# A gated feed-forward layer in seven-product form: the last product of the first down projection divided once more

## The chip, the cores and the metric

One NeuronCore of a Trainium2 chip runs the whole kernel; there is no other core in it. The metric is the device time of one launch in microseconds. Before the change three runs gave 529.53, 529.77 and 530.21 us, median 529.77.

## The reference

```
def reference(x, w_gate, w_up, w_down):
    g = jnp.einsum("bsd,df->bsf", x, w_gate)
    u = jnp.einsum("bsd,df->bsf", x, w_up)
    h = _gelu(g) * u
    return jnp.einsum("bsf,fd->bsd", h, w_down)
```

x has 2048 rows of 1024 columns, the hidden width is 3584, all in bf16; `_gelu` is the tanh form. Three large matrix products, then, with a gate between the second and the third.

## The kernel before

**Seven products for eight.** A product of two matrices cut into 2 x 2 blocks is done with seven block products instead of eight. Sums of blocks of the left matrix (s1 to s4) and of the right one (t1 to t4) are made ahead, seven products are taken of blocks and sums, and the results are put together with adds. Sums are kept in a 32-bit form (`fp32r`), in which the matmuls then run.

**First part, up to about 350 us.** Gate and up projections, in two halves of 1024 rows (`NPASS` = 2, each of two blocks of 512 rows), over 28 blocks of 128 hidden columns. Here nearly all blocks are cut a second time, and GpSimd makes most of the sums. The products h leave for DRAM (`hd`), and sums of blocks of w_down too (`td`), since SBUF can't hold them.

**Second part: `down`, twice.** `down(0, ...)` does the first 1024 rows of the output, `down(1, ...)` the last 1024. In each, the left matrix h is four blocks h00, h01, h10, h11 (`h[kh][c]`: kh the half of the hidden width, c the block of 512 rows), each 14 tiles (`NJ`) of 128 hidden columns by 512 rows. Its stages follow each other on TensorE:
- two raw products in bf16, h00 and h10 with the raw left columns of w_down (`chunk`, `rows`, L707 to L733); the raw columns come in chunks of two tiles: `fetch12` puts one chunk into a slot, `fetch_early` four chunks into one of the two `w` tiles.
- two products of sums, s2 with t2 and s1 with t1 (L735 to L744); VectorE makes s1 and s2 (`make12`), t1 and t2 are loaded from `td` (`load12`).
- two more, s3 with t3 and s4 with the raw right columns (L746 to L757); VectorE makes s3, t3 and s4 (`make73`), from raw columns that `fetch73` loads; ACT casts the raw ones (`tb`).
- the last product, the block h11 with t4, which is loaded from `td` by `load4`.

Only the last stage differs between the two calls. In the first, h11 is cast on ACT tile by tile (`make_sa`), and 14 tiles by four row blocks, 56 matmuls of 512 columns, go into the banks `e`, which ACT then copies out (`put21`, L759). In the second, `inner_product` (L638) cuts this product once more into seven, over 7 tiles (`H`) and 256 columns (`Q`): each of the seven is 14 matmuls of 256 columns, 98 in all. Its left sums s1 to s4 are four VectorE adds of 128 x 1792 (`inner_sums`), of which s1 and s2 lie in the tiles `xT` and s3 and s4 in the two `w` tiles. Its right sums are 28 GpSimd adds of 128 x 256: `inner_t` (t1, then t2 from it, seven times), `inner_t3` (seven) and `inner_t4` (seven). `inner_cast` casts h11 on ACT.

**What sets the order.** SP (which issues all DMAs), VectorE, GpSimd and TensorE run in the order in which the code is written (`tc.manual_schedule`), and every wait holds up all that stands behind it on its engine. In `down`, `step(n)` is called ahead of each piece of TensorE's work and runs what an agenda has for that n: `at` holds for both halves, `at_tail(last, ...)` for one. So `at_tail(1, 50 + 1.3 * t, inner_t, t)` puts the sums of tile t at step 50 + 1.3t of the second half. `more_0` has the loads of h for the second half, at steps 56, 59, 61 and 63 of the first, and the two `fetch_early` at step 46.

**Room.** 59 slots of 2 KB per partition (`kpool`) are handed out in turn; a tile that gets a slot waits until its last reader is done. The `w` pool has two tiles. SP has at most eight DMAs under way: each waits for the landing of the eighth before it. `even`, `odd`, `cc`, `dd` are pairs of the eight PSUM banks; `e` and `c` of `down` are four banks each, and change places between the halves.

All DVE sums go through `dve` (L94), all GpSimd sums through `pool` (L97), all matmuls of this part through `matmul` (L115), so these are the lines that the profile names; tiles tell them apart.

```
def dve(out, a, b, op):
    nc.vector.tensor_tensor(out=out, in0=a, in1=b, op=op)

def pool(out, a, b, op):
    nc.gpsimd.tensor_tensor(out=out, in0=a, in1=b, op=op)
```

Of the kernel before, what the change touches and what calls it, by code (L numbers as in the profile page):

```python
# [10 lines left out]
def kernel(  # L11
# [10 lines left out]
    nc = tc.nc  # L22
    ENG = mybir.EngineType
    ORDER = {ENG.SP, ENG.DVE, ENG.Pool, ENG.PE}
    P = nc.NUM_PARTITIONS
# [15 lines left out]
    NJ = NFB // 2  # L41
# [14 lines left out]
    AT12 = [0, 0, 1, 2, 4, 5, 9, 12, 16, 18, 22, 27, 29, 31], [4, 4, 8, 8, 12, 12, 15, 16, 18, 20, 22, 27, 29, 31]  # L56
    AT12S = [6, 7, 9, 10, 13, 14, 16, 18, 20, 23, 25, 27, 29, 31]
    EARLY = 8
    AT73 = [31 + 2 * j if j < 7 else 38 + j for j in range(NJ)]

    ctx.enter_context(tc.manual_schedule(engines=ORDER))
# [472 lines left out]
        tb = cast(rr[:, 1, :], "tb")  # L534
        q73[j] = s3, t3, s4, tb

    def make_sa(j):
        sa[j] = cast(h[1][1][:, j, :], "sa")

    def fetch12(n):  # L540
        kh, j = n // 7, 2 * (n % 7)
        if (1, n) in raw:
# [10 lines left out]
            raw[1, n] = big[:, n - n0]  # L553
            nc.sync.dma_start(out=raw[1, n], in_=wdn[:, kh, j : j + 2, :N])

    def inner_sums(late):
        hi = h[1][1][:, :H], h[1][1][:, H:]
        a11, a21 = hi[0][:, :, :Q], hi[0][:, :, Q:]
        a12, a22 = hi[1][:, :, :Q], hi[1][:, :, Q:]
        if not late:  # L560
            s1, s2 = [xpool.tile([P, H, Q], f32r, name=f"xT{n}") for n in range(2)]
            dve(s1, a21, a22, ADD)
            dve(s2, s1, a11, SUB)
            return s1, s2
        s3, s4 = [wpool.tile([P, H, Q], f32r, name="w") for _ in range(2)]
        dve(s3, a11, a21, SUB)
        dve(s4, a12, inner[1], SUB)
        return s3, s4

    def inner_t(t):  # L570
        b1, b2 = q4[t], q4[H + t]
# [27 lines left out]
    for j in range(NJ):  # L599
        at(AT12S[j], make12, j)  # L600
        at(AT73[j] - 4, fetch73, j)
        at(AT73[j], make73, j)
    sa, it, inner = {}, {}, []
    tails = {}, {}

    def at_tail(last, step, what, j):
# [4 lines left out]
    for j in range(NJ):  # L611
        for last in range(2):
            if last or j not in STAY:
                at_tail(last, AT12[last][j], lambda j, last=last: load12(j, BIG12[last]), j)
        at_tail(0, 49 + 0.65 * j, load4, j)
        at_tail(0, 54 + 0.55 * j, make_sa, j)
    for t in range(H):
        for j in (t, H + t):
            at_tail(1, 47 + 1.3 * t, load4, j)
        at_tail(1, 50 + 1.3 * t, inner_t, t)  # L620
        at_tail(1, 59, inner_t3, t)
        at_tail(1, 60, inner_t4, t)
        at_tail(1, 53 + 1.1 * t, inner_cast, t)

    def load_h(p, kh, c, j0, j1):
        nc.sync.dma_start(out=h[kh][c][:, j0:j1], in_=hd[p, kh, c][:, j0:j1])
# [8 lines left out]
        r0 = (2 * ip + c) * N + i * P  # L635
        nc.sync.dma_start(out=out2[r0 : r0 + P, dc * N : (dc + 1) * N], in_=st)

    def inner_product(ip, e, c, ss):  # L638
        zz = [hpool.tile([P, 2, N], f32, name=f"h{n}0") for n in range(2)]
        z1, z6, z7, z5 = [b.rearrange("p (r q) -> p r q", r=2) for b in c]  # L640
        T = range(H)
        a11 = [sa[t] for t in T]
        a12 = [sa[H + t][:, :Q] for t in T]
        a22 = [sa[H + t][:, Q:] for t in T]
        b11, b21 = [[q4[h + t][:, :Q] for t in T] for h in (0, H)]
        b22 = [q4[H + t][:, Q:] for t in T]
        t1, t2, t3, t4 = [[it[t][n] for t in T] for n in range(4)]
        s1, s2, s3, s4 = [[s[:, t] for t in T] for s in ss]

        def go(out, lhs, rhs, fresh=False, rs=R2):  # L650
            for r in rs:
                for t in T:
                    matmul(
                        out(r), lhs[t][:, r * P : (r + 1) * P], rhs[t],
                        fresh and r == 0 and t == 0, t == H - 1,
                    )

        left, right = slice(0, Q), slice(Q, N)

        def put(i):  # L660
            r0 = (2 * ip + 1) * N + i * P
            st = slot([P, N], bf16, "st")
            dve(st, e[i], zz[i // 2][:, i % 2], ADD)
            nc.sync.dma_start(out=out2[r0 : r0 + P, :N], in_=st)

        go(lambda r: e[r][:, right], s4, b22, rs=range(1))
        go(lambda r: z1[:, r], a11, b11, True)
        nc.scalar.copy(out=zz[0][:, :, left], in_=z1)
        go(lambda r: z6[:, r], s2, t2, True)
        u2 = new(dve, z6, zz[0][:, :, left], ADD, "sum", [P, 2, Q], f32)  # L670
        go(lambda r: z7[:, r], s3, t3, True)
        dve(zz[1][:, :, left], z7, u2, ADD)
        go(lambda r: z5[:, r], s1, t1, True)
        dve(zz[0][:, :, right], z5, u2, ADD)
        go(lambda r: e[r][:, right], s4, b22, rs=range(1, 2))
        go(lambda r: e[r][:, left], a12, b21, rs=range(1))
        put(0)
        dve(zz[1][:, :, right], z5, zz[1][:, :, left], ADD)
        go(lambda r: e[r][:, left], a12, b21, rs=range(1, 2))
        put(1)  # L680
        for r in R2:
            go(lambda r: e[2 + r][:, left], a22, t4, rs=range(r, r + 1))
            put(2 + r)

    def down(ip, e, c, last, more):
        I = range(NS)

        def step(n):
            todo(n, last)
            if last and n in (20, 44):  # L690
                inner.extend(inner_sums(n == 44))
            more(n)

        def chunk(kh, j):
            n = kh * 7 + j // 2
            got = raw[1, n][:, j % 2, :]
            if j % 2:
                raw.pop((1, n))
            return got

        def rows(ps, lhs, rhs, start, stop, some=I):
            for i in some:
                matmul(ps[i], lhs[:, i * P : (i + 1) * P], rhs, start, stop)

        step(-1)
        held = []
        for j in range(NJ):  # L707
            step(j)
            held.append((j, chunk(0, j)))
            if j < NJ - SEAM and (last or j >= SEAM):  # L710
                for some in (I[:2], I[2:]):
                    for k, rhs in held:
                        rows(e, h[0][0][:, k, :], rhs, k == 0, False, some)
                held = []
        for i in I:
            for k, rhs in held:
                rows(e, h[0][0][:, k, :], rhs, False, k == NJ - 1, [i])
            nc.scalar.copy(out=c[i], in_=e[i])
        held = []
        for j in range(NJ):  # L720
            step(NJ + j)
            held.append((j, chunk(1, j)))
            if j == 1:
                for i in I:
                    for k, rhs in held:
                        rows(c, h[1][0][:, k, :], rhs, False, False, [i])
            if j > 1:
                for k, rhs in held:
                    rows(c, h[1][0][:, k, :], rhs, False, k == NJ - 1)
            if j > 0:  # L730
                held = []
        for i in I:
            store(ip, 0, i, 0, lambda st: nc.scalar.copy(out=st, in_=c[i]))  # L733

        for t in range(NJ + LAG):  # L735
            step(2 * NJ + t)
            if t < NJ:
                rows(e, s12[t][1], q12[t][1], False, t == NJ - 1)
            if t == NJ - 1:
                u2 = [snap(e[i], "u2") for i in I]  # L740
            if t >= LAG:
                j = t - LAG
                rows(c, s12[j][0], q12.pop(j)[0], j == 0, j == NJ - 1)
        p5 = [snap(c[i], "p5") for i in I]  # L744

        for t in range(NJ + LAG):  # L746
            step(3 * NJ + LAG + t)
            if t < NJ:
                rows(e, q73[t][0], q73[t][1], False, t == NJ - 1)
            if t == NJ - 1:  # L750
                for i in I:
                    store(ip, 1, i, 1, lambda st: dve(st, e[i], p5[i], ADD))
            if t >= LAG:
                j = t - LAG
                rows(c, q73[j][2], q73[j][3], False, j == NJ - 1)
        for i in I:
            store(ip, 0, i, 1, lambda st: dve(st, c[i], u2[i], ADD))  # L757

        def put21(i):  # L759
            store(ip, 1, i, 0, lambda st: nc.scalar.copy(out=st, in_=e[i]))  # L760

        if last:
            for j in range(NJ):
                step(4 * NJ + 2 * LAG + j)
            inner_product(ip, e, c, inner)
        else:
            for j in range(NJ):
                step(4 * NJ + 2 * LAG + j)
                rows(e, sa[j], q4[j], False, j == NJ - 1)
            for i in I:  # L770
                put21(i)


    warm = nc.const_aps.tensor(1.0, [P, N], bf16)
# [346 lines left out]
    def more_0(step):  # L1121
# [2 lines left out]
            load_h(0, 1, 1, 8, NJ - 1)  # L1124
        if step == 32:
            store_made(NJ - 1)
        if step in (56, 59, 61):
            kh, c = {56: (0, 0), 59: (1, 0), 61: (0, 1)}[step]
            new_h(kh, c)
            for j0, j1 in ((0, 4), (4, 8), (8, NJ)):  # L1130
                load_h(1, kh, c, j0, j1)
        if step == 46:
            fetch_early(0), fetch_early(4)
        if step == 63:
            new_h(1, 1)
            for j0, j1 in ((0, 4), (4, 8), (8, NJ)):
                load_h(1, 1, 1, j0, j1)

    E = [E[0][1], E[0][0], E[1][0], E[1][1]]
    down(0, E, F[0] + F[1], False, more_0)  # L1140
    down(1, F[0] + F[1], E, True, lambda step: None)

# [28 lines left out]
```

## Time and profile before

| | us |
|---|---|
| median of three runs | 529.77 |
| the profiled execution | 528.81 |
| its span, first to last instruction | 527.0 |
| TensorE busy | 520.1 |
| VectorE busy | 384.8 |
| GpSimd busy | 329.6 |
| ACT busy | 290.9 |
| second part, first half begins | 349 |
| its last product, begin and end | 424.07, 436.76 |
| second half's last product begins | 511.75 |

The span is 1.8 us shorter than the execution's time, which has a start and an end around it. The granted TensorE clock is 0.999 of full speed over the span. The 16 DMA engines are busy nearly without a break from 399 us to 471 us, at up to 420 GB/s.

How to read the lines: PE is TensorE's matmuls, PEld its weight loads, DVE VectorE, POOL GpSimd, SPq the DMA issues of SyncE. A line of the timeline gives start, length, engine, line of the code, operation, output <- inputs by the names of the tiles, shape, and how many instructions were put together in it; in brackets how long the engine was idle before and what ended that. Recorded lengths of matmuls overlap: the distance of their starts tells what one costs. Recorded lengths of VectorE and GpSimd adds overlap a little too, by 0.04 to 0.09 us where one follows another at once.

### The profile page before, as it was taken

To read this page: it belongs to the slowest core of one execution; us is meant where nothing else is said; L and a number is where in the kernel's file an instruction comes from. 1 tells how busy PE (TensorE), PEld (TensorE's weight loads), DVE (VectorE), ACT (ScalarE), POOL (GpSimd) and SP (SyncE) were. 2 spreads that over 40 slices of the span, in tenths; PEclk is the share of its full clock that TensorE was granted. 3 is DMA by queue.
4 is the path that set the end of the run, shared out by engine and by line. 5 is a ranking of instruction groups with operands and counts; after the bars stand their busy time and mean duration, and the time that the engine had idled before them with its cause. 6 is when DMAs were issued, how large, how long until landed. Compare 5 with 4: busy or idle time off the path is not lost.

```text
span 527.0 us, 7930 instructions
## 1 busy us (share of the span) xinstructions
PE 520.1 (99%) x2362; PEld 368.4 (70%) x2393; DVE 384.8 (73%) x586; ACT 290.9 (55%) x535; POOL 329.6 (63%) x339
## 2 busy tenths in 40 slices
PE   8999999999999999999999999999999999999997
PEld 4568686867667676767676676754788884488887
DVE  2984636427889889898978889897789226976933
ACT  2555655656778687868787786851135602133430
POOL 1179959998899999999999999840000000000494
PEclk9999999999999999999999999999999999999999
DMA  9785244131625357363827455999997999983741
GB/s 249 160 191 125 76 131 119 41 109 58 204 80 180 108 194 222 111 205 126 255 91 229 148 173 159 332 372 416 385 294 224 400 350 375 394 297 113 227 135 61
DMA packets 104906, 106.96 MB, mean 203 GB/s; under 512 B 19744, under 2 KB 82976, under 8 KB 104864
## 3 DMA queue, kind: packets, MB, share of 16 engines
q1 hardware_dynamic: 104864, 106.46, 62.1%
q8 instruction: 19, 0.31, 0.2%
q14 instruction: 23, 0.19, 0.1%
HBM read 73.66 MB, written 29.62 MB: 196 GB/s over the span
## 4 chain that ended last, share of the span: by engine, by line
PE 96%; DMA 2%; DVE 1%; issue 0%; SPq 0%; ACT 0%; ACTq 0%; DVEq 0%
PE bank L115 96%; DMA hd<-h 1%; DMA xn<-in_x_dram 1%; DVE bank L94 0%; SPq L783 0%; DVE h L94 0%; DVE kz L94 0%; DVE st L94 0%; PE bank L790 0%; ACT u L111 0%; ACT ky L111 0%; DVE v L94 0%; ACTq L111 0%; DVEq L94 0%
## 5 line engine op out<-in xcount | busy, mean ns | idle before, releaser
L115 PE MATMUL bank<-h,s 128*128 128x512 f32 x492 | 129.3, 394 | 0.0
L97 POOL TENSOR_TENSOR q<-q 128x256 fp32r<-128x256 f32 x28 | 24.3, 901 | 145.9 <-PE bank L115 145.4
L115 PE MATMUL bank<-xT,w 128*128 128x512 bf16 (+1 forms) x448 | 106.0, 376 | 1.4
L115 PEld LDWEIGHTS bank<-h,s 128*128 128x128 f32 x492 | 92.3, 188 | 20.9 <-ACT u L111 0.5
L115 PEld LDWEIGHTS <-w 128*128 128x128 bf16 x504 | 45.7, 98 | 59.0 <-issue 10.6
L97 POOL TENSOR_TENSOR s<-w 128x512 fp32r<-128x512 bf16 (+1 forms) x74 | 75.9, 1041 | 17.6 <-DMA w<-in_w_gate_dram 10.5
L115 PE MATMUL bank<-t,s 128*128 128x512 f32 x276 | 75.5, 399 | 0.3 <-ACT u L111 0.3
L115 PE MATMUL bank<-q 128*128 128x512 f32 x264 | 65.6, 390 | 0.0
L115 PEld LDWEIGHTS bank<-t,s 128*128 128x128 f32 x276 | 51.6, 188 | 12.8 <-ACT u L111 1.0
L111 ACT COPY p<-bank 128x512 f32<-128x512 f32 x76 | 42.8, 588 | 29.2 <-PE bank L115 28.6
L115 PEld LDWEIGHTS bank<-q 128*128 128x128 f32 x264 | 49.6, 188 | 10.4
L111 ACT COPY u<-bank 128x512 f32<-128x512 f32 x62 | 36.0, 592 | 30.4 <-PE bank L115 27.7
L94 DVE TENSOR_TENSOR q<-h,h 128x512 fp32r<-128x512 bf16 x56 | 38.4, 685 | 15.4 <-DMA h<-hd 15.4
L97 POOL TENSOR_TENSOR s<-s,s 128x256 fp32r<-128x256 f32 x57 | 42.2, 762 | 1.5
L115 PEld LDWEIGHTS <-h 128*128 128x128 bf16 x224 | 21.7, 98 | 26.5 <-issue 0.5
L94 DVE TENSOR_TENSOR xz<-bank,xz 128x512 f32<-128x512 f32 x40 | 27.5, 691 | 16.9 <-PE bank L115 11.0
L97 POOL TENSOR_TENSOR s<-w,s 128x512 fp32r<-128x512 bf16 (+1 forms) x36 | 39.1, 1102 | 0.6 <-ACT sh L106 0.6
L97 POOL TENSOR_TENSOR s<-s,w 128x512 fp32r<-128x512 f32 (+1 forms) x36 | 36.6, 1035 | 0.8
L97 POOL TENSOR_TENSOR m<-raw,m 128x512 fp32r<-128x512 bf16 x28 | 34.5, 1232 | 2.2
L106 ACT CAST tb<-raw 128x512 fp32r<-128x512 bf16 x28 | 16.8, 632 | 30.7 <-DMA raw<-in_w_down_dram 23.9
L94 DVE TENSOR_TENSOR h<-g,bank 128x512 bf16<-128x512 f32 x42 | 28.6, 685 | 6.7 <-ACT g L209 3.5
L94 DVE TENSOR_TENSOR bank<-bank,u 128x512 f32<-128x512 f32 x47 | 32.4, 688 | 0.0
(117 smaller groups left out, 907.9 us busy)
## 6 DMA issues: line engine op xcount, KB each, us to landing
raw<-in_w_down_dram SPq DMA_DIRECT2D x68, 256.0 KB, 3.9
q<-td SPq DMA_DIRECT2D x66, 256.0 KB, 5.4
hd<-h SPq DMA_DIRECT2D x110, 128.0 KB, 1.7
td<-m SPq DMA_DIRECT2D x42, 256.0 KB, 2.3
h<-hd SPq DMA_DIRECT2D x17, 512.0 KB, 6.9
out_dram<-st SPq DMA_DIRECT2D x32, 128.0 KB, 3.6
h<-hd SPq DMA_DIRECT2D x5, 768.0 KB, 9.4
w<-in_w_gate_dram SPq DMA_DIRECT2D x7, 512.0 KB, 4.4
```

The lines of the kernel that those rows point to most:

```text
L94: nc.vector.tensor_tensor(out=out, in0=a, in1=b, op=op)
L97: nc.gpsimd.tensor_tensor(out=out, in0=a, in1=b, op=op)
L106: nc.scalar.copy(out=t, in_=src)
L111: nc.scalar.copy(out=t, in_=ps)
L115: nc.tensor.matmul(ps, lhsT=lhs, rhs=rhs, start=start, stop=stop, skip_group_check=True)
```

## The change

The first half's last product takes the form of the second's: 98 matmuls of 256 columns through `inner_product`, with a branch of its own there, instead of 56 of 512.
- Sums: `load4`, `inner_t`, `inner_t3`, `inner_t4` and `inner_cast` now stand on both agendas, at the same steps; `make_sa` and `put21` go. `inner_sums` becomes `inner_sum(n)`, one sum per call. In the first half sums 0 and 1 are made at step 54, 2 and 3 inside `inner_product`, between VectorE's adds there. In the second half they stay at steps 20 and 44.
- Partial results (`zz`) of the first half go into four slots instead of two `h` tiles, and `put` adds each output block in two halves of 256 columns.
- Loads for the second half: the two `fetch_early` at step 46 become four `fetch12` at step 55. `fetch_early(4)`, the loads of h01 and h11 and three further `fetch12` are issued by `late_loads`, inside `inner_product`, where the tile of sum 2 has to come free first. The loads of h00 and h10 stay at steps 56 and 59.
- Order of the seven in the first half: a12 b21, a11 b11, s2 t2, s1 t1, s3 t3, s4 b22, a22 t4.

```diff
+    INNER = {54: (0, 1)}, {20: (0, 1), 44: (2, 3)}
...
-        at_tail(0, 49 + 0.65 * j, load4, j)
-        at_tail(0, 54 + 0.55 * j, make_sa, j)
     for t in range(H):
+        for last in range(2):
+            for j in (t, H + t):
+                at_tail(last, 47 + 1.3 * t, load4, j)
+            at_tail(last, 50 + 1.3 * t, inner_t, t)
+            at_tail(last, 59, inner_t3, t)
+            at_tail(last, 60, inner_t4, t)
+            at_tail(last, 53 + 1.1 * t, inner_cast, t)
...
+            zz = [[slot([P, 2, Q], f32, "z") for _ in R2] for _ in R2]
...
+                for n in R2:
+                    dve(st[:, sides[n]], e[i][:, sides[n]], zz[i // 2][n][:, i % 2], ADD)
...
+        if not ip:
+            go(lambda r: e[r][:, left], a12, b21)
+            go(lambda r: z1[:, r], a11, b11, True)
+            nc.scalar.copy(out=zz[0][0], in_=z1)
+            go(lambda r: z6[:, r], s2, t2, True)
+            inner_sum(2)
+            u2 = new(dve, z6, zz[0][0], ADD, "sum", [P, 2, Q], f32)
+            inner_sum(3)
+            go(lambda r: z5[:, r], s1, t1, True)
+            dve(zz[0][1], z5, u2, ADD)
+            go(lambda r: z7[:, r], s3, t3, True)
+            dve(zz[1][0], z7, u2, ADD)
+            late_loads()
+            dve(zz[1][1], z5, zz[1][0], ADD)
+            go(lambda r: e[r][:, right], s4, b22)
+            for i in range(2):
+                put(i)
+            for r in R2:
+                go(lambda r: e[2 + r][:, left], a22, t4, rs=range(r, r + 1))
+                put(2 + r)
+            return
...
-        if step == 46:
-            fetch_early(0), fetch_early(4)
+        if step == 55:
+            for n in range(4):
+                fetch12(n)
...
+    def late_loads():
+        fetch_early(4)
+        for kh in range(2):
+            new_h(kh, 1)
+            for j0, j1 in ((0, 4), (4, 8), (8, NJ)):
+                load_h(1, kh, 1, j0, j1)
+        for n in range(EARLY, EARLY + 3):
+            fetch12(n)
```

More of the change, by code (lines that the diff above doesn't have):

```diff
@@ L535, in make73 @@
         q73[j] = s3, t3, s4, tb
-    def make_sa(j):
-        sa[j] = cast(h[1][1][:, j, :], "sa")
     def fetch12(n):
@@ L554, in fetch_early, with inner_sum @@
             nc.sync.dma_start(out=raw[1, n], in_=wdn[:, kh, j : j + 2, :N])
-    def inner_sums(late):
+    def inner_sum(n):
         hi = h[1][1][:, :H], h[1][1][:, H:]
@@ L559, in inner_sums @@
         a12, a22 = hi[1][:, :, :Q], hi[1][:, :, Q:]
[L560 to L568, printed above, removed]
+        if n < 2:
+            inner[n] = xpool.tile([P, H, Q], f32r, name=f"xT{n}")
+        else:
+            inner[n] = wpool.tile([P, H, Q], f32r, name="w")
+        a, b, op = ((a21, a22, ADD), (inner[0], a11, SUB), (a11, a21, SUB), (a12, inner[1], SUB))[n]
+        dve(inner[n], a, b, op)
     def inner_t(t):
@@ L602 @@
         at(AT73[j], make73, j)
-    sa, it, inner = {}, {}, []
+    sa, it, inner = {}, {}, [None] * 4
     tails = {}, {}
@@ L614 @@
                 at_tail(last, AT12[last][j], lambda j, last=last: load12(j, BIG12[last]), j)
-        at_tail(0, 49 + 0.65 * j, load4, j)
-        at_tail(0, 54 + 0.55 * j, make_sa, j)
     for t in range(H):
[L618 to L623, printed above, removed]
+        for last in range(2):
[5 more added lines that the diff above has]
+            at_tail(last, 53 + 1.1 * t, inner_cast, t)
     def load_h(p, kh, c, j0, j1):
@@ L636, in store, with inner_product @@
         nc.sync.dma_start(out=out2[r0 : r0 + P, dc * N : (dc + 1) * N], in_=st)
-    def inner_product(ip, e, c, ss):
-        zz = [hpool.tile([P, 2, N], f32, name=f"h{n}0") for n in range(2)]
+    def inner_product(ip, e, c):
+        if ip:
+            z = [hpool.tile([P, 2, N], f32, name=f"h{n}0") for n in range(2)]
+            zz = [[t[:, :, :Q], t[:, :, Q:]] for t in z]
+        else:
+            zz = [[slot([P, 2, Q], f32, "z") for _ in R2] for _ in R2]
         z1, z6, z7, z5 = [b.rearrange("p (r q) -> p r q", r=2) for b in c]
@@ L647, in inner_product @@
         t1, t2, t3, t4 = [[it[t][n] for t in T] for n in range(4)]
-        s1, s2, s3, s4 = [[s[:, t] for t in T] for s in ss]
+        s1, s2, s3, s4 = range(4)
         def go(out, lhs, rhs, fresh=False, rs=R2):
+            if isinstance(lhs, int):
+                lhs = [inner[lhs][:, t] for t in T]
             for r in rs:
@@ L658, in inner_product @@
         left, right = slice(0, Q), slice(Q, N)
+        sides = left, right
         def put(i):
@@ L662, in put @@
             st = slot([P, N], bf16, "st")
-            dve(st, e[i], zz[i // 2][:, i % 2], ADD)
-            nc.sync.dma_start(out=out2[r0 : r0 + P, :N], in_=st)
+            if ip:
+                dve(st, e[i], z[i // 2][:, i % 2], ADD)
+            else:
+                for n in R2:
+                    dve(st[:, sides[n]], e[i][:, sides[n]], zz[i // 2][n][:, i % 2], ADD)
+            nc.sync.dma_start(out=out2[r0 : r0 + P, :N], in_=st)
+        if not ip:
[19 more added lines that the diff above has]
+            return
         go(lambda r: e[r][:, right], s4, b22, rs=range(1))
         go(lambda r: z1[:, r], a11, b11, True)
-        nc.scalar.copy(out=zz[0][:, :, left], in_=z1)
+        nc.scalar.copy(out=zz[0][0], in_=z1)
         go(lambda r: z6[:, r], s2, t2, True)
-        u2 = new(dve, z6, zz[0][:, :, left], ADD, "sum", [P, 2, Q], f32)
+        u2 = new(dve, z6, zz[0][0], ADD, "sum", [P, 2, Q], f32)
         go(lambda r: z7[:, r], s3, t3, True)
-        dve(zz[1][:, :, left], z7, u2, ADD)
+        dve(zz[1][0], z7, u2, ADD)
         go(lambda r: z5[:, r], s1, t1, True)
-        dve(zz[0][:, :, right], z5, u2, ADD)
+        dve(zz[0][1], z5, u2, ADD)
         go(lambda r: e[r][:, right], s4, b22, rs=range(1, 2))
@@ L677, in inner_product @@
         put(0)
-        dve(zz[1][:, :, right], z5, zz[1][:, :, left], ADD)
+        dve(zz[1][1], z5, zz[1][0], ADD)
         go(lambda r: e[r][:, left], a12, b21, rs=range(1, 2))
@@ L689, in step @@
             todo(n, last)
-            if last and n in (20, 44):
-                inner.extend(inner_sums(n == 44))
+            for some in INNER[last].get(n, ()):
+                inner_sum(some)
             more(n)
@@ L757, in down @@
             store(ip, 0, i, 1, lambda st: dve(st, c[i], u2[i], ADD))
[L759 to L771, printed above, removed]
+        for j in range(NJ):
+            step(4 * NJ + 2 * LAG + j)
+        inner_product(ip, e, c)
     warm = nc.const_aps.tensor(1.0, [P, N], bf16)
@@ L1126, in more_0 @@
             store_made(NJ - 1)
-        if step in (56, 59, 61):
-            kh, c = {56: (0, 0), 59: (1, 0), 61: (0, 1)}[step]
-            new_h(kh, c)
+        if step in (56, 59):
+            kh = int(step == 59)
+            new_h(kh, 0)
             for j0, j1 in ((0, 4), (4, 8), (8, NJ)):
-                load_h(1, kh, c, j0, j1)
-        if step == 46:
-            fetch_early(0), fetch_early(4)
-        if step == 63:
-            new_h(1, 1)
+                load_h(1, kh, 0, j0, j1)
+        if step == 55:
+            for n in range(4):
+                fetch12(n)
+    E = [E[0][1], E[0][0], E[1][0], E[1][1]]
+    def late_loads():
+        fetch_early(4)
+        for kh in range(2):
+            new_h(kh, 1)
             for j0, j1 in ((0, 4), (4, 8), (8, NJ)):
-                load_h(1, 1, 1, j0, j1)
-    E = [E[0][1], E[0][0], E[1][0], E[1][1]]
+                load_h(1, kh, 1, j0, j1)
+        for n in range(EARLY, EARLY + 3):
+            fetch12(n)
     down(0, E, F[0] + F[1], False, more_0)
```

## The prediction

> **What bounds the kernel now.** I read the page first (busy shares, then the chain that ended last), then the timeline of each engine from 395 us on, where the change lies, then the landings of the DMAs there.
>
> ```profile
> PE 520.1 (99%) x2362; PEld 368.4 (70%) x2393; DVE 384.8 (73%) x586; ACT 290.9 (55%) x535; POOL 329.6 (63%) x339
> PE 96%; DMA 2%; DVE 1%; issue 0%; SPq 0%; ACT 0%; ACTq 0%; DVEq 0%
> ```
>
> TensorE is the bound: 99% busy, 96% of the chain, and its timeline shows no idle time from 350 us to 523 us. So a matmul removed is time won, and any wait put into TensorE's queue is time lost at full price. The stage that changes is the last product of the first half, 424.07 to 436.76, 12.69 us; the form it takes on is that of the last product of the second half.
>
> ```profile
> 420.44 3.79 PE L115 MATMUL bank<-tb,q 128*128 128x512 f32 x16
> 424.07 12.85 PE L115 MATMUL bank<-q,sa 128*128 128x512 f32 x56
> 436.76 13.99 PE L115 MATMUL bank<-w,h 128*128 128x512 bf16 x62
> ```
> ```profile
> 511.75 0.99 PE L115 MATMUL bank<-q,w 128*128 128x256 f32 x7
> 512.58 1.84 PE L115 MATMUL bank<-q,sa 128*128 128x256 f32 x14
> ...
> 520.03 3.52 PE L115 MATMUL bank<-q,sa 128*128 128x256 f32 x28
> ```
>
> Starts are what count in these rows: 56 matmuls of 512 columns in 12.69 us are 0.227 each. In the second half 98 matmuls of 256 columns begin at 511.75 and the last one begins at 520.03 + 3.52 - 0.28 (its own length) = 523.27: 97 steps in 11.52 us, 0.119 each, a little over half of 0.227.
>
> **Part 1, TensorE's work.** 56 x 0.227 = 12.69 us go, 98 x 0.1188 = 11.64 us come: **-1.05 us**, and no more than that is to be had. Without any new wait the products would begin at: a12*b21 424.1, z1 425.7, z6 427.4, z5 429.1, z7 430.7, s4*b22 432.4, a22*t4 434.0, end 435.7.
>
> **Part 2, the sums on GpSimd.** The 28 sums of `inner_t`, `inner_t3`, `inner_t4` are new in this half, where GpSimd is idle from 349 us on. They are those of the second half, which the trace shows. From the second sum on (500.09) to the end of the last (519.65) they take 19.56 us: 1.51 per pair while t2 waits for t1, 0.70 each for the 14 of t3 and t4, 0.74 for one alone. The first one is the row that decides this case:
>
> ```profile
> 494.76 5.25 POOL L97 TENSOR_TENSOR q<-q 128x256 fp32r<-128x256 f32 x1 [145.35 <-PE bank L115]
> ```
> ```profile
> 498.13 0.69 DVE L94 TENSOR_TENSOR q<-raw 128x512 fp32r<-128x512 bf16 x1
> 498.73 0.69 DVE L94 TENSOR_TENSOR q<-h,q 128x512 fp32r<-128x512 bf16 x1
> ```
>
> It takes 5.25 us instead of 0.74. VectorE then runs the sums of `make73`, one every 0.60 us without a gap, each with both inputs in SBUF, and ends at 499.41; GpSimd's sum ends 0.60 us behind that. So GpSimd did not get in while they ran. The reverse is seen where the first projections run:
>
> ```profile
> 155.25 2.29 POOL L97 TENSOR_TENSOR s<-s,w 128x512 fp32r<-128x512 f32 x2
> 156.39 1.70 DVE L94 TENSOR_TENSOR h<-v,v 128x512 bf16<-128x512 f32 x1
> 157.50 1.61 POOL L97 TENSOR_TENSOR s<-w,s 128x512 fp32r<-128x512 bf16 x1
> ```
>
> `h<-v,v` (two SBUF inputs) needs 0.69 alone; here it ends 0.55 behind the GpSimd sum that was running (157.54), and the next GpSimd sum is 0.5 longer than its usual 1.1. One waits for the other; VectorE adds that read PSUM, such as the one at 158.01, run beside GpSimd.
>
> When may GpSimd start? In the built program its first sum waits for a buffer that matmul 32 of the 112 of the stage before frees: 398.67 + 32 x 0.227 + 0.2 = 406.1 (in the second half it is matmul 36: 486.35 + 36 x 0.227 + 0.2 = 494.7; the row says 494.76). The q loads that it reads land earlier than it needs them: the loads of the stage no longer stand behind eight `w` loads (398.83 to 403.21 on SP). From 406.1 I add up what the two engines must do one at a time:
> - the rest of `make73` on VectorE, 406.1 to 410.1: 4.0
> - `inner_sum(0)` and `(1)`, put right behind it: 2 x 2.02 (the `xT<-h` rows at 451.25 and 453.31), 4.05
> - the 28 GpSimd sums, 0.74 + 19.56 = 20.3
> - `inner_sum(2)` and `(3)`, which the change sets **between** the products on VectorE, behind the u stores (426.07) and behind u2 (429.9): 4.05.
>
> 406.1 + 32.4 = **438.5** for the last t4 sum. Who gets in first does not change this sum. In order of time: second GpSimd sum at 414.8, t2 complete at 424.6 (needed 427.4), five t3 sums by 430.1 around `inner_sum(2)`, then `inner_sum(3)` to 432.1, the last t3 at 433.5, t4 433.5 to 438.4. In the second half none of this hurts, since all four inner sums are over at 486.8, before GpSimd starts.
>
> **TensorE behind it.** z7 begins at 430.7, waits for t3 until 433.5 and ends at 434.5 instead of 432.4. s4*b22 runs to 436.2 (its `inner_sum(3)` is there at 432.1). a22*t4 takes its seventh matmul after 438.4 and then seven more: 438.4 + 0.12 + 0.83 = **439.4**. The second half so begins 2.65 us later than at 436.76.
>
> **Part 3, loads, queue, the rest.** SP's queue now holds `late_loads` until z7 has ended (the tile of `inner_sum(2)` has to come free): 434.6. Behind it wait four chunks of w_down, six of h, three more chunks. From an idle queue the first lands 2.5 us after issue (471.14 to 473.8); then a landing each 0.70 us for 256 KB, 1.27 for 512 KB, 1.9 to 2.45 for 768 KB (landings between 403 and 442). Chunk 8 lands at 434.6 + 2.5 + 3 x 0.70 + 9.5 + 0.70 = 449.4; TensorE wants it 13.83 us into the half (450.59 - 436.76), at 453.2: 3.8 us of cover. The first `make12` starts some 7 us later than its 438.85, its product is wanted at 463.4. With what stands behind on the queue the first raw chunk of `make73` lands near 471 instead of 464.7, that is 3.6 us later against TensorE; VectorE has 3.70 us idle to give:
>
> ```profile
> 482.03 2.02 DVE L94 TENSOR_TENSOR w<-h 128x1792 fp32r<-128x1792 bf16 x1 [3.70 <-PE bank L115]
> ```
>
> So nothing, or under 0.5 us. The four casts `st` on ACT become eight VectorE adds of 128x256, which no row of before shows on VectorE: between half of 0.69 and 0.69 each; they end by 441, and their banks are wanted 10.4 us into the half (447.17 - 436.76). If that cover went, each would cost its length. The z copy on ACT (0.59) ends before u2 wants it; the `sa` casts go from 14 to 11, beside TensorE.
>
> **Sum.** 436.76 becomes 439.4: +2.65. On the profiled execution, 528.81 (span 527.0 and 1.8 around it), that is 531.5; it was 0.96 under the median of the three runs, 529.77, so **532.4**. The boundaries (up to 0.74 where each inner sum meets a GpSimd sum, both ways) make it 531.7 to 533.2.
>
> **Rivals.**
> 1. *Not slower: the sums get through in time.* The 5.25 us could be a start after 145 us of rest and not a wait. Then GpSimd's last sum ends at 406.1 + 5.25 + 19.56 = 430.9, no product waits, and 528.7 comes out. It decides by the last t4 sum: by 434.8 the whole gain stays, at 435.8 nothing is won. Against it: the end 0.60 behind VectorE's last sum, and `h<-v,v`. [...]
> 2. *VectorE kept out of GpSimd's run.* The t3 and t4 sums come without a gap as `make73` does. If `inner_sum(2)` had to wait for all 14 (424.6 + 9.8 = 434.4), z7 starts at 436.4, `inner_sum(3)` ends at 439.1, the stage at 442.4: +5.7, 535.4. Against it: at 157.54 VectorE got in though GpSimd's next sum had been issued at 157.50.
> 3. *The late loads are late.* Without the wait of the forecast their cover is 2.1 us (447.4 for 449.5). Should the six h loads take half as long again (+4.7), 528.7 + 2.6 = 531.3; with the wait 532.4 + 0.9 = 533.3.
> 4. *The clock falls in the gaps.* TensorE waits 3.7 us in pieces of at most 1.6. No row shows a lower clock (0.999). If the clock halved for as long as it had waited, the second half would begin with 3.7 us at half speed: +1.9, 534.3. [...]
>
> **Chances.** Forecast 0.70, rival 1 0.10, rival 2 0.08, rival 3 0.07, rival 4 0.05. The range 530.8 to 534.4 holds the forecast, rivals 3 and 4, and leaves out rivals 1 and 2 (0.18). A measurement of this kernel can tell about 0.2% (1.06 us) from no change; rival 1 lies right at that bound and is halved: faster 0.06, same 0.06, slower 0.88.
>
> **What would show it.** Right: the first GpSimd sum near 406 several us long; `inner_sum(2)` and `(3)` each longer than 2.02 or a GpSimd sum near them about 2.7; TensorE idle in z7 (about 2 us) and in a22*t4 (about 2) behind GpSimd; the stage 15.3 us long; no idle time in the second half. Wrong: 28 sums of 0.74 from 406 on; TensorE idle near 450 behind a DMA; a granted clock under 1.

## The result, and the profile after

Five runs of the changed kernel have a median of 533.41 us (532.52 to 533.70), five of the kernel before 529.53 (528.33 to 530.21): ratio **1.0071**, 95% interval 1.0057 to 1.0086, so 3.0 to 4.6 us slower. Compared again it was 532.87 against 529.24, ratio 1.0067 (1.0045 to 1.0088). The forecast was 532.4, between 530.8 and 534.4.

The profiled execution took 533.51 us, its span is 531.4. From the page, the same two lines that were shown of before:

```profile
PE 521.7 (98%) x2404; PEld 371.0 (70%) x2435; DVE 396.9 (75%) x602; ACT 288.3 (54%) x529; POOL 363.1 (68%) x367
PE 87%; POOL 6%; DVE 3%; DMA 2%; issue 1%; ACT 0%; POOLq 0%; DVEq 0%; ACTq 0%
```

The chain that ended last was 96% TensorE; now 6% of it are GpSimd (4% the sums `q` of the change) and 3% VectorE. TensorE's waits from 420 us on (engine, line, waited for: us in all, times, longest), of which the kernel before had none:

```profile
PE bank L116 <- POOL q L98: 2.2, 5, 1.0
```

The pauses recorded are shorter than what they cost, since recorded lengths of matmuls overlap (the first row below ends at 428.97, the next begins at 428.80); the cost is read from starts. Where they are, the timeline of TensorE says. The first half's last product:

```profile
425.45 3.52 PE L116 MATMUL bank<-q,sa 128*128 128x256 f32 x28
428.80 3.44 PE L116 MATMUL bank<-q,xT 128*128 128x256 f32 x28
432.07 0.88 PE L116 MATMUL bank<-q,w 128*128 128x256 f32 x6
433.96 2.90 PE L116 MATMUL bank<-q,w 128*128 128x256 f32 x22 [1.02 <-POOL q L98]
436.70 1.14 PE L116 MATMUL bank<-q,sa 128*128 128x256 f32 x5
438.14 0.38 PE L116 MATMUL bank<-q,sa 128*128 128x256 f32 x1 [0.30 <-POOL q L98]
438.82 1.22 PE L116 MATMUL bank<-q,sa 128*128 128x256 f32 x8 [0.30 <-POOL q L98]
439.88 7.08 PE L116 MATMUL bank<-raw,h 128*128 128x512 bf16 x31
```

and the second half's:

```profile
514.88 0.99 PE L116 MATMUL bank<-q,w 128*128 128x256 f32 x7
...
520.20 0.38 PE L116 MATMUL bank<-q,w 128*128 128x256 f32 x1 [0.30 <-POOL q L98]
520.89 1.22 PE L116 MATMUL bank<-q,w 128*128 128x256 f32 x8 [0.30 <-POOL q L98]
...
524.41 3.52 PE L116 MATMUL bank<-q,sa 128*128 128x256 f32 x28
```

Three differences make up the 4.4 us between the two spans:
- the first half's last product takes 439.88 - 425.45 = 14.43 us, before 12.69: **+1.74** (forecast +2.65);
- the second half's takes 524.41 - 514.88 = 9.53 from its first row to its last, before 8.28: **+1.25** (forecast nothing);
- the stage began at 425.45 instead of 424.07: 1.38. From the begin of the second part (350.5 us, before 349.1) to this stage both take 75.0 us, so this lies in the first part, where the two kernels have the same code.

Between the two products TensorE takes 75.0 us in both kernels.

The two products, +3.0 together, also are the difference of the spans where more executions are counted: in the second comparison the median spans are 530.4 and 527.5. The times lie further apart, 3.6 to 3.9 us, since part of the loss stands outside the span: in every execution of the kernel before whose span is on record the time is 1.7 to 1.8 us longer than the span, in the 13 of the changed kernel 2.1 to 2.9 us. No trace shows what this is; with t3 on VectorE (below) it is 1.7 to 1.8 again.

**The first half.** GpSimd's first sum, which was issued at 407.56, and three others, each from its own narrow window of the timeline (left out are the ordinary ones, 0.74 each):

```profile
407.56 6.30 POOL L98 TENSOR_TENSOR q<-q 128x256 fp32r<-128x256 f32 x1 [56.00 <-DMA q<-td]
...
413.94 2.40 POOL L98 TENSOR_TENSOR q<-q 128x256 fp32r<-128x256 f32 x1
...
427.44 2.53 POOL L98 TENSOR_TENSOR q<-q 128x256 fp32r<-128x256 f32 x1
...
431.34 2.57 POOL L98 TENSOR_TENSOR q<-q 128x256 fp32r<-128x256 f32 x1
```
```profile
411.24 2.02 DVE L95 TENSOR_TENSOR xT<-h 128x1792 fp32r<-128x1792 bf16 x1
413.29 2.45 DVE L95 TENSOR_TENSOR xT<-xT,h 128x1792 fp32r<-128x1792 f32 x1
...
427.37 2.01 DVE L95 TENSOR_TENSOR w<-h 128x1792 fp32r<-128x1792 bf16 x1
...
431.31 2.01 DVE L95 TENSOR_TENSOR w<-h,xT 128x1792 fp32r<-128x1792 bf16 x1
```

The second view is VectorE's. Four GpSimd sums are long, and each lies beside one of the four VectorE adds of 128 x 1792; the first also beside the rest of `make73`, and it ends 0.60 us behind the add at 411.24.

**The second half.** VectorE's rows of `make73` and the two adds in the midst of it:

```profile
473.90 0.69 DVE L95 TENSOR_TENSOR q<-raw 128x512 fp32r<-128x512 bf16 x1 [3.82 <-DMA raw<-in_w_down_dram]
...
482.27 0.69 DVE L95 TENSOR_TENSOR q<-raw 128x512 fp32r<-128x512 bf16 x1 [1.48 <-DMA raw<-in_w_down_dram]
...
488.90 2.02 DVE L95 TENSOR_TENSOR w<-h 128x1792 fp32r<-128x1792 bf16 x1
```

It waits for raw columns twice, and the 3.70 us of idle time that stood ahead of `w<-h` before are gone.

### The profile page after: what moved, and what is told of

Same layout as the page of the kernel before. It is cut to its first block, busy times and chain, and to the rows that moved or that the text cites. A ratio compares the mean times of both kernels' runs of the same rounds, so it can differ in the third digit from the quotient of the medians.

```text
span 531.4 us, 8064 instructions
## 1 busy us (share of the span) xinstructions
PE 521.7 (98%) x2404; PEld 371.0 (70%) x2435; DVE 396.9 (75%) x602; ACT 288.3 (54%) x529; POOL 363.1 (68%) x367
## 4 chain that ended last, share of the span: by engine, by line
PE 87%; POOL 6%; DVE 3%; DMA 2%; issue 1%; ACT 0%; POOLq 0%; DVEq 0%; ACTq 0%
PE bank L116 86%; POOL q L98 4%; DMA hd<-h 2%; DVE bank L95 1%; DVE h L95 1%; PE bank L865 1%; DMA raw<-in_w_down_dram 1%; POOL s L98 1%; PE bank L807 0%; POOL n L98 0%; POOL m L98 0%; POOL h L98 0%; DVE v L95 0%; DVE kz L95 0%; POOLq L1189 0%
## 5 line engine op out<-in xcount | busy, mean ns | idle before, releaser
L98 POOL TENSOR_TENSOR q<-q 128x256 fp32r<-128x256 f32 x56 | 57.9, 1067 | 116.3 <-PE bank L116 59.2
L116 PE MATMUL bank<-raw,h 128*128 128x512 bf16 x156 | 34.7, 379 | 0.2
```

The costliest lines, as they stand in the source:

```text
L116: nc.tensor.matmul(ps, lhsT=lhs, rhs=rhs, start=start, stop=stop, skip_group_check=True)
```

## The experiments

**Two theories.** T1: VectorE adds with two inputs in SBUF and GpSimd's adds take turns, and this sum, too long by the four inner sums, makes the first product late. T2: the late loads make `make73` late, this keeps GpSimd out for longer, and its t3 sums come late in the second product. Against both stands one rival each: that the waits have another cause, and the time does not move when the suspect is taken away. "First product" is the first half's last product from here on, "second product" the second half's.

| kernel | first product | second, first to last row | sum against before | ratio (interval) |
|---|---|---|---|---|
| before | 12.69 | 8.28 | | |
| changed | 14.43 | 9.53 | +2.99 | 1.0071 (1.0057 to 1.0086) |
| changed, again | 14.59 | 9.44 | +3.06 | 1.0067 (1.0045 to 1.0088) |
| all four inner sums ahead | 14.35 | 8.83 | +2.21 | 1.0059 (1.0040 to 1.0078) |
| sums 2, 3 off VectorE | 11.66 | 10.25 | +0.94 | 1.0031 (1.0014 to 1.0048) |
| h01 early | 14.41 | 8.29 | +1.73 | 1.0039 (1.0023 to 1.0056) |
| t3 on VectorE, first half | 11.66 | 9.66 | +0.35 | 1.0021 (1.0008 to 1.0033) |
| both mends | 11.71 | 9.69 | +0.43 | 0.9996 (0.9986 to 1.0007) |
| and five t3 in the second half | 11.71 | 8.28 | -0.98 | 0.9979 (0.9965 to 0.9992) |
| and all seven | 11.99 | 10.31 | +1.33 | 0.9997 (0.9984 to 1.0010) |

Products are of the one profiled execution, in us; ratios are of medians; 0.2% is 1.06 us. The profiled execution was the fastest of its seven for t3 on VectorE, and the slowest of its twelve for both mends and for all seven, so a product and a ratio of one row need not agree.

**Is it a sum, or where the adds stand?**

```diff
-    INNER = {54: (0, 1)}, {20: (0, 1), 44: (2, 3)}
+    INNER = {54: (0, 1, 2, 3)}, {20: (0, 1), 44: (2, 3)}
...
-            inner_sum(2)
...
-            inner_sum(3)
```


> All four inner sums of the first half stand at step 54, behind make73; none is left between the products. Theory (VectorE adds with two SBUF inputs and GpSimd adds take turns, so only their sum counts): nothing is won. The second GpSimd sum starts about 419.4 instead of 415.6 (in the profile's time of the changed kernel), the last t4 sum ends at 438.8 to 439.5, the first half's last product takes 14.4 to 15.2 us against 14.43, the time is that of the changed kernel, 533.4, to 0.8 above. Rival (it is the place of the sums between the products that costs): the product falls to 11.6 to 12, the time by 2.5 to 2.8, to about 530.7.

532.13 us against 529.39, and a first product of 14.35, just under the 14.4 to 15.2 of the theory and far from the rival's 11.6 to 12. The time is lower than the theory had, by the profile because the second product waited only 0.55 us. The last GpSimd sum ends 13.2 us behind the product's begin, as in the changed kernel (13.3). So it matters little where the adds stand. The second GpSimd sum was expected at 419.4, behind all four adds, and that was wrong: it was issued at 412.90. The GpSimd sums that wait now follow one another, the first four in a row; the first three of them in the timeline (the fourth took 2.39):

```profile
406.40 6.42 POOL L98 TENSOR_TENSOR q<-q 128x256 fp32r<-128x256 f32 x1 [56.78 <-DMA q<-td]
412.90 2.41 POOL L98 TENSOR_TENSOR q<-q 128x256 fp32r<-128x256 f32 x1
415.26 2.52 POOL L98 TENSOR_TENSOR q<-q 128x256 fp32r<-128x256 f32 x1
```

VectorE's second, third and fourth adds took 2.45, 2.56 and 2.55 beside them instead of 2.02, with no more than 0.04 us between them: one GpSimd sum between two VectorE adds, turn by turn. The last two of these rows show turns of one instruction each: a sum of 0.74 ends 2.4 to 2.5 us after its issue, beside an add of 2.0. The first does not: that sum stayed out for a whole run of adds, 6.42 us, not for one (see the last section).

**Without the two adds.**

```diff
+        if n > 1 and not late_done:
+            nc.scalar.copy(out=inner[n], in_=a)
+            return
         dve(inner[n], a, b, op)
```


> Leaves out the subtraction in sums 2 and 3 of the first half: ACT copies one of their blocks into the same tiles at the same place of the code, so every wait on those tiles stays, and VectorE has no add there. Theory (turns): GpSimd gains the two holds of 1.8 us, its last t4 sum ends near 435.2 instead of 438.76, when a22*t4 would begin at 435.4; the first half's last product falls from 14.43 to 11.7 to 12.2, the time to 530.8 to 531.3. Rival (GpSimd starts late after its rest and needs its 20 us whatever VectorE does): the last sum stays at 438.8, the product at 14.4, the time at 533.4.

530.97 us, as T1 has it; the first product takes 11.66 us with no wait, a little under the 11.7 expected, and 11.64 was the prediction's figure for 98 matmuls. GpSimd's run is 27.60 us instead of 31.21, so the two adds had cost it 1.8 us each. But the second product's wait grew to 10.25 - 8.28 = 1.97: TensorE is ahead by 2.8 us, the loads are not.

**One of the late loads back in its place.**

```diff
+        if step in (56, 59, 61):
+            kh, c = {56: (0, 0), 59: (1, 0), 61: (0, 1)}[step]
```


> h01 is loaded at step 61 as before the change; late_loads keeps the rest. Theory for the second half (late loads make make73 late on VectorE, and that keeps GpSimd out longer): the first half's last product stays at 14.4; the first raw chunk of make73 lands some 4 us earlier, VectorE ends make73 3 us earlier, the second half's last product falls from 12.77 to 11.5 to 11.7, the time by 1.1 to 1.25, to about 532.2. Rival (GpSimd's second-half sums wait for a matmul to free their buffer, as 36 matmuls into the stage shows): 12.8 stays, 533.4.

531.40 us. The second product has no wait (8.29), the first is as it was (14.41): T2 holds: the second cost goes and the first stays. The time is lower than the 532.2 expected, though the first raw columns of `make73` came only 2.4 us earlier against TensorE, where some 4 were expected. What the load's place does to the 16 DMA engines is in two stretches of the trace (columns: stretch, its length, busy time and count of PE, PEld, DVE, ACT, POOL, then the clock, the DMA share and GB/s). Of the changed kernel:

```profile
430.00:435.00 5.00, 3.98 (x34) 3.78 (x33) 3.22 (x3) 0.00 (x0) 5.00 (x5) 1.00 0.61 225
435.00:440.00 5.00, 4.29 (x31) 3.63 (x30) 3.46 (x8) 0.00 (x0) 3.77 (x6) 1.00 0.69 207
```

and with h01 early:

```profile
430.00:435.00 5.00, 3.98 (x33) 3.77 (x33) 3.61 (x5) 0.00 (x0) 5.00 (x6) 1.00 1.01 404
435.00:440.00 5.00, 4.31 (x27) 3.06 (x26) 3.46 (x9) 0.00 (x0) 2.68 (x4) 1.00 1.04 332
```

While SP stands at `late_loads` (it waits 5.8 us there for TensorE), the DMA engines run empty for about a third of 10 us. From 440 to 480 us they are at 0.98 to 1.06 in the changed kernel, so what was lost there comes back nowhere: `make73` gets its first raw columns 34.0 us into the second half, with h01 early 31.6, before 28.05.

As much is lost ahead of the stage. In the three stretches of 5 us from 400 to 415 us the DMA share is 0.61, 0.89 and 0.80 in the changed kernel (0.62, 0.88 and 0.74 with h01 early), and 0.93, 1.01 and 1.05 before: there the `w` loads of the two `fetch_early` are gone from step 46. Added up, each of the two gaps is 3.5 us of the DMA engines' time; together they come near the 7.7 us by which the first raw columns of `make73` are later, counted from the stage's begin (48.4 us, before 40.7).

**t3 of the first half on VectorE**, in its idle time of 5.6 us ahead of the p stores:

```diff
-            at_tail(last, 59, inner_t3, t)
+            if last:
+                at_tail(last, 59, inner_t3, t)
+            else:
+                at_tail(last, 57, lambda t: inner_t3(t, dve), t)
```


> The changed kernel, with the seven t3 sums of the first half made by VectorE in its idle time ahead of the p stores instead of by GpSimd; nothing is left out. Theory (the two engines' adds add up): GpSimd loses 7 x 0.70 = 4.9 us of its run and is kept out for 7 x 0.35 = 2.5 more, so its last t4 sum ends 10.9 us behind the begin of the stage instead of 13.3, z7 does not wait, a22*t4 a little; the stage takes 11.9 to 12.1 us instead of 14.43. Second theory (late loads): the loads are issued about 1.2 us later against the second half's begin, make73 ends later by as much, and the wait in the second half grows from 1.25 to between 1.6 and 2.0 us. Together 1.7 to 2.0 us under the changed kernel. Rival (the adds of VectorE are kept out by GpSimd's run, or keep it out for longer than they last): the stage stays at 14 us or more, and the time at the changed kernel's.

The first product takes 11.66 and has no wait; GpSimd's run is 27.33 us instead of 31.21, 3.9 less (2.4 expected: seven t3 sums on VectorE cost GpSimd less than 0.35 each). The second product's wait is 1.38; "1.6 to 2.0" was a little too much. All in all 530.48, which is 2.4 us under the changed kernel of the same comparison (1.7 to 2.0 expected).

**Both mends.**

> The changed kernel with both mends: t3 of the first half on VectorE, and h01 loaded at step 61 as before. If both theories hold, the first half's last product takes 11.9 to 12.1 us (12.69 before) and the second half's has no wait (first to last row 8.29 us, as before): 0.6 to 0.8 us under the kernel before by the stages, which is at the edge of what can be told; some 3 us under the changed kernel. Rival (the two costs are one, and the other appears when one goes): a wait of over 1 us behind GpSimd in the second half's last product, and a time not under the kernel before's.

529.29 against 529.24: the gain of the first half is there (11.71), but the second product waits 1.41 us all the same. So the expectation failed in its second half. With h01 early alone nothing waited; there the first product, and TensorE behind it, was 2.7 us later. And here the place of h01 brought the raw columns of `make73` no further forward: they come 47.0 us behind the stage's begin, as with t3 on VectorE alone. With both mends the DMA engines are at 0.92 to 1.07 from 420 to 480 us, but still at 0.55, 0.93 and 0.75 from 400 to 415. No run puts the `fetch_early` back at step 46, so what that place alone costs stays open. The wait in the second product follows one quantity in all profiles so far, the end of GpSimd's first sum there, counted from the product's begin:

| kernel | end of that sum | wait of the product |
|---|---|---|
| before | -11.74 | 0 |
| h01 early | -11.73 | 0 |
| four sums ahead | -9.50 | 0.55 |
| changed, again | -8.89 | 1.16 |
| changed | -8.79 | 1.25 |
| t3 on VectorE | -8.66 | 1.38 |
| both mends | -8.64 | 1.41 |
| sums 2, 3 off VectorE | -8.07 | 1.97 |

It is 10.04 us plus that place in every kernel that waits; so the kernel before had 1.7 us to give. And that sum ends 0.6 us behind the last add of `make73`, whatever its length (5.25 before, 8.14 changed).

**t3 in the second half too**, five of the seven (the first condition), or all (the second):

```diff
-            if last:
+            if last and t > 4:
```
```diff
-            if last:
+            if last and t > 6:
```


> The kernel with both mends, and in the second half too five of the seven t3 sums on VectorE, behind make73 and ahead of the p stores. In all profiles so far the wait in the second half's last product is 10.0 us plus the place (negative) at which GpSimd's first sum ends against the product's begin: -11.7 gives none, -8.65 gives 1.4. If that wait is GpSimd's run being too long for its late begin, the run loses 5 x 0.55 = 2.75 us (in the first half seven such sums shortened it by 3.87), the wait goes, and the two products take 11.7 and 8.3 us, 20.0 against 21.0 of the kernel before: 1.0 us under it, ratio 0.998. Rival: the adds on VectorE push its p and u stores, and with them the banks that z1 and z6 want; they should end at 507.5, 0.6 ahead of the p stores, so this would show as a wait of TensorE behind VectorE in the second half.

> As the one before, with all seven t3 sums of the second half on VectorE. By the same theory no wait behind GpSimd either, but VectorE's seven adds last 6.2 us (as in the first half), until 509.3, which is 1.2 us into its p stores: the u stores come 1.2 us late, and z1 waits up to 0.5 us for its bank. So 0 to 0.5 us above the one before. If the stores have cover that I don't see, the same time.

With five, 528.10 us against 529.29, ratio 0.9979 (0.9965 to 0.9992): the only kernel here whose interval lies under the one before. TensorE waits for nothing after 420 us; its first product runs from 423.78 to 435.49, and of its second these are the first and the last row:

```profile
510.48 1.00 PE L116 MATMUL bank<-q,w 128*128 128x256 f32 x7
...
518.76 3.52 PE L116 MATMUL bank<-q,sa 128*128 128x256 f32 x28
```

That is the whole gain of Part 1 of the prediction, 1.0 us, and no wait of TensorE behind VectorE shows, which was the rival. With all seven, 529.40, which is 1.3 us more where 0 to 0.5 was expected, and not for the reason given: VectorE's seven adds were over at 507.13, ahead of its stores, and it is GpSimd's first sum, the longest of all, that is late; TensorE waits for t2. GpSimd's row, and the third of the seven products on TensorE:

```profile
494.77 12.09 POOL L98 TENSOR_TENSOR q<-q 128x256 fp32r<-128x256 f32 x1 [63.80 <-PE bank L116]
```
```profile
514.21 0.74 PE L116 MATMUL bank<-q,xT 128*128 128x256 f32 x5
...
516.82 1.20 PE L116 MATMUL bank<-q,xT 128*128 128x256 f32 x8 [1.10 <-POOL q L98]
```

Six t3 adds followed `make73` on VectorE without a break there, and GpSimd got in only when the seventh had to wait 0.24 us for its load. The median is lower than the products of this profile would make it (+0.1 us against before, not +1.3), so VectorE's run was probably broken earlier in other executions; no trace of one shows it.

**The 1.38 us ahead of the stage.**

> The changed kernel once more, for its time on the same chip as the others and for where its first half's last product begins. If the 1.38 us by which it began later in the first profile belong to the change, it begins again at 425 or later; if they are the spread of executions, it begins between 423.5 and 425. The stage takes 14.4 us, and the second half's last product 9.0 to 9.6 from first to last row, either way.

> The kernel before, a second profile. The changed kernel's first half's last product began at 425.45 instead of 424.07, though the code ahead of it is the same. If that 1.38 us is the spread of executions, this second profile shows a start anywhere from 423.5 to 425.5; if it belongs to the changed kernel, this one starts at 424.1 and each of the variants of the changed kernel near 425.4.

> The kernel before once more, for where its first half's last product begins. Nine profiles of kernels with the change began it between 423.6 and 426.9 (mean 424.8), two of the kernel before at 423.5 and 424.1. If the later begin is the spread of executions, this one may lie anywhere in 423.5 to 426; if it belongs to the change, it lies at 424.1 or earlier.

> The same, a further execution: anywhere in 423.5 to 426 if it is spread; 424.1 or earlier again if it belongs to the change.

The changed kernel began its stage at 424.82 this time, and the kernel before at 423.48, 424.87 and 424.67. So most of it is spread of executions: four profiles of before lie between 423.5 and 424.9, nine with the change between 423.6 and 426.9, and TensorE's waits there change from one to the next (for x, for `u`, for `s`). The means are 424.3 and 424.8; whether that half microsecond belongs to the change can't be told from these.

## Why the prediction was right, and where it was not

The time lay 1.0 us above the forecast and inside its range. The mechanism of the larger term was right, but that the time came so close is in part luck: two terms were off in opposite directions, the first product by 0.9 us too much and the second by 1.25 too little, and they nearly cancel. The prediction also carried the 1.8 us outside the span over unchanged; it was 2.1 to 2.9.

- **TensorE's work, -1.05:** right. Without waits 98 matmuls take 11.66 us (11.64 forecast), and the kernel with five t3 sums moved gains just this.
- **The two engines add up:** right as a mechanism, 1.2 us too long. From the issue of GpSimd's first sum to the end of its last, 32.4 us were forecast and 31.21 measured. The rest of `make73` took 3.68 instead of 4.0, and the four adds cost GpSimd 1.88 (6.30 - 3.68 - 0.74), 1.66, 1.79 and 1.83 instead of 2.02 each: 0.9 less, so an add that is recorded as 2.01 does not hold the other engine up for all of it. The 28 sums themselves: 27.60 - 3.68 - 1.88 - 1.66 = 20.38 in the run without sums 2 and 3; 20.3 was the forecast. So z7 waited 1.0 us, not 2, and the stage grew by 1.74, not 2.65.
- **Order of the turns:** VectorE was to make both inner sums ahead of GpSimd's second sum; GpSimd got its first in between them, and its second behind them. As the prediction said, this didn't change the sum.
- **Late loads, "nothing, or under 0.5":** this step failed; it was 1.25 us (1.16 in the second profile). Its lag was too small: the first raw columns of `make73` came 6.0 us later against TensorE (34.0 - 28.05), not 3.6. Of these 2.4 us 0.9 are TensorE, which lost less in the first product than forecast; the other 1.4 are the loads, 7.7 us later against the stage's begin where 6.3 were forecast, in a stretch in which the DMA engines were full again after the two gaps. And the cover was taken from the wrong place. VectorE's 3.70 us were used up, its last add of `make73` came 3.0 us later against TensorE (505.50 - 439.88 = 65.62, before 499.41 - 436.76 = 62.65), and on that end hangs GpSimd's first sum, by the very row of 5.25 us on which Part 2 was built. Of the 3.0 GpSimd had 1.7 to give; 1.25 came through.
- **Rival 1** (a start cost of 5.25): fell. The first sum in the second half took from 5.19 to 12.09 us, always until just behind VectorE. **Rival 2** (VectorE kept out for GpSimd's run): fell; `inner_sum(2)` got in at the end of the sum in progress (it began at 427.37, that sum at 426.74, and the next, at 427.44, took 2.53). **Rival 3**: TensorE did not wait for a load near 450; chunk 8 landed at 451.95, wanted at 453.7, so 1.75 us of its cover of 3.8 were left. The loads were late at another place, through two engines. **Rival 4**: in the traces of the kernel before and of the changed one the granted clock is 1.00 up to the last matmul, in the changed one through waits of up to 1.02 us in the two products. It falls only behind it, to 0.50: 2.6 us after the last matmul's recorded end before (526.2 against 523.55), 3.2 in the changed kernel (531.1 against 527.93). The waits are shorter than either; with the longest of all profiles, 1.18 us in the changed kernel's second, the mean clock of that execution is 0.999. Two of the five executions of the changed kernel show a mean clock of 0.996 and 0.997; their spans (530.9 and 531.0) are no longer than those of the others (530.4 to 531.6), and no trace shows where in them it fell.
- **"No idle time in the second half"** was the sign to look at: the waits at 520.20 and 520.89 were what told this term apart.

## What to carry to other kernels

When a late load is costed at nothing because an engine has idle time, follow that engine's end to whoever waits for it, and count the cover of each link: here 3.70 us on VectorE and 1.7 on GpSimd. For a bound, add up VectorE's adds with two SBUF inputs and GpSimd's adds as one queue; here that bound was 1.2 us of 32.4 too long. VectorE's adds that read a PSUM bank stay out of it: the four of the p stores took 2.48 us beside GpSimd's sums (at 421.34), and as much in the kernel before, where GpSimd was idle (at 419.96). Moving a sum to the engine where it is shorter can pay even where both are busy: seven t3 sums, 0.70 each on GpSimd and 0.35 on VectorE (six in 2.10 us where GpSimd was kept out), shortened GpSimd's run by 3.9 us in the first half. Moving all seven in the second half lost again what five had won, by its profile since they lengthened the run of adds that kept GpSimd out. A stage that gets shorter does not take its loads along: with the first product 2.7 us shorter (both mends against h01 early) the DMA engines stayed full, and the wait came back in the second product.

## What the runs showed of the hardware beyond that

**Who gets in.** A run of VectorE adds without a break kept GpSimd out as a whole, not add by add: 5.19 to 12.09 us for a sum of 0.74 in the second half, until 0.6 us behind the run. One short break ended it: 0.24 us with all seven t3 sums there, and in the first half of the changed kernel the 0.03 us between the two adds into `xT`. With five t3 sums it ended behind the first of them (GpSimd's sum took until 502.15, the t3 adds began at 501.14). With both mends one add of `make73` in the first half had to wait 0.20 us for a matmul; VectorE's rows there:

```profile
408.40 0.69 DVE L95 TENSOR_TENSOR q<-h,q 128x512 fp32r<-128x512 bf16 x1
409.30 0.94 DVE L95 TENSOR_TENSOR q<-h,h 128x512 fp32r<-128x512 bf16 x1 [0.20 <-PE bank L116]
410.16 1.22 DVE L95 TENSOR_TENSOR q<-raw 128x512 fp32r<-128x512 bf16 x1
```

GpSimd's first sum was done after 2.16 us instead of 6.3, and from then on the two went one for one: the adds of `make73` show 1.22 instead of 0.69, the GpSimd sums 1.07 to 1.18. Why the first entry needed a break and the later ones did not, no run here tells.
